# Batch 0 of a sparse-attention kernel: loads, casts and scores taken pair by pair, in one written order

## The chip, the cores and the metric

The kernel runs on one core of one Trainium2 chip. Its metric is device time in microseconds, the median of three runs. The core's engines are TensorE (PE, with its weight loads shown as PEld), VectorE (DVE), ScalarE (ACT), GpSimd (POOL) and SyncE (SP), which issues most of the DMAs. Each engine works through its own instructions in order; engines wait for one another by semaphores.

## The reference

Eight batches of eight heads, 576 tokens, 64 values a head, all float32. Heads 0 to 3 see the last 32 positions, heads 4 to 7 the earlier positions with the same remainder by 32. A feed-forward part without nonlinearity, but with a product of two branches, follows.

```python
scores = scale * np.matmul(q, k.transpose(0, 1, 3, 2))
mask_local = (rel >= 0) & (rel < stride)                       # heads 0..3, stride 32
mask_strided = (rel >= 0) & (pos[None, :] % stride == pos[:, None] % stride)   # heads 4..7
scores = np.where(masks, scores, -1e9)
attn = softmax(scores)                                         # max taken off, divided by the sum
attn_out = np.matmul(attn, v)                                  # (8, 8, 576, 64)
x = attn_out.transpose(0, 2, 1, 3).reshape(4608, 512)
out = ((x @ w1) * (x @ w2)) @ w3 @ w_out                       # 512 -> 1024 -> 1024 -> 512
```

## The kernel before

Work is cut into pairs of heads: 4 pairs in each of 8 batches, 32 in all. Pairs 0 and 1 of a batch are local (`s.local`, blocks of 96 queries, six of them), pairs 2 and 3 strided. In the first two batches (`AHEAD = 2`) strided pairs are in a "natural" layout (`s.nat`): token 4p+c is row p of block c, and the last 64 tokens (the "rest", loaded apart by `load_rest`) make a fifth block. For a pair the steps are:

- load q and k (`load_qk`: four heads, 512 KB a DMA, from SP), cast them to fp16,
- T1: four 128x128 PE transposes each for q and k (`ah_T1`), copied out of PSUM to `qT` by ACT and to `kT` by DVE (`ah_T1c`); `ah_R` does the rest of all pairs,
- scores in two groups. In batch 0 a bias matmul puts a large negative number where the mask is 0 (`ah_bias`, `biasL` and `biasN`), the score matmuls add to it (`ah_S0`), and ACT's exponential writes `ptm` or `nptm`. For natural pairs ACT also copies the last 16 columns to `emb` (`ah_tail`),
- PV (`ah_PV`): the weights times v with a column of ones, so that the sum comes along; `norm` on DVE takes a reciprocal of the sum and multiplies, for each of the two groups, into `xqs`,
- T2 (`ph_T2`): PE transposes of `xqs`, copied out to `xT` by ACT; for natural pairs DVE copies the last 64 columns.

Values: `load_vL` loads them for local pairs, casts them and copies 32 rows of each block's neighbour (the "halo") on POOL; `load_vN` does the strided ones. The columns of ones and the zero rows of `v16L` and `v16X` are memsets.

The feed-forward part works on tiles of 512 tokens. For each of eight column blocks jc, `a` makes x@w1 (PSUM tile `aps`, four matmuls over the four pairs' `xT`, ci = 0..3), ACT copies it to `asb`, `bb` makes x@w2 (`bps`), and DVE multiplies the two into `abt`. w3 and w_out are folded into one matrix on the core (`fold_tr`, `fold_tr2`: transposes of w3; `fold_mm`: the products, PSUM tile `ops`), so that one more matmul gives the output (`o_parts`). Weights are loaded by SP through the nine staging buffers of pool `stgp` and cast on POOL.

PE's order is written by hand: `pe(...)` holds an instruction in program order. For the other engines a scheduler places instructions, unless they are held too; `behind(x)` makes an instruction be issued after x. The list `stream` holds the steps of batch 0 in order, then those of batches 2 to 7 with gaps, which `host` fills with feed-forward work. In batch 0 before, T1, scores, PV and T2 of the four pairs are interleaved, and the first 16 `a` matmuls of the feed-forward part (four blocks, four ci) are set between the PV and T2 steps of the later pairs. Then come the `bb` matmuls of four blocks, the other blocks, the fold (with batch 1's steps at set places, `plan`), and from pair 8 on the batches of the `stream`. Pair 8 and 9 are the local pairs of batch 2.

PSUM is held by three pools: `psF` (three banks), `psB` (two tiles of two banks, for scores and shared `a` tiles) and `psM` (one bank). `warm(ps, n)` issues n 128x128 matmuls whose result nobody reads.

Of the kernel before, what the change touches and what calls it, by code (L numbers as in the profile page):

```python
# [19 lines left out]
def kernel(  # L20
# [64 lines left out]

    def copy(eng, out, in_):
        if eng == "a":
            return nc.scalar.copy(out=out, in_=in_)  # L88
        elif eng == "v":
            return nc.vector.tensor_copy(out=out, in_=in_)  # L90
        return nc.gpsimd.tensor_copy(out=out, in_=in_)  # L91
# [4 lines left out]
    make_identity(nc, id16)  # L96


# [6 lines left out]
    tmp2 = att.tile([P, 2 * S], FP16, tag="pte", bufs=2, name="tmp2")  # L105
    causal = tmp[:, 0:NW]
    nc.gpsimd.memset(causal, 1.0)
    nc.gpsimd.affine_select(out=causal, in_=causal, compare_op=ALU.is_ge,
                            fill=0.0, base=0, pattern=[[1, NW]], channel_multiplier=-1)
    setup["p"] = nc.gpsimd.affine_select(out=maskE[:, 0:P], in_=causal[:, 0:P], compare_op=ALU.is_ge,  # L110
                                         fill=0.0, base=31, pattern=[[-1, P]], channel_multiplier=1)
    nptms = [ffn.tile([P, 2, 2048], FP16, tag="abt", bufs=4, name="nptm0")]
    nc.gpsimd.memset(emb, 0.0)

    mps = psF.tile([P, 512], FP32, tag="f")
    sels = []
    for m, lo, n, w in ((8, 208, 18, P), (32, 352, 2, 64), (7, 0, 18, XW), (4, P, 18, YW)):
        sel = tmp[0:m, NW + lo:NW + lo + n * m]
        nc.vector.tensor_copy(out=sel.rearrange("r (t a) -> r t a", a=m),
                              in_=_ap(id16, 0, [[id16.ap[0][0], m], [0, n], [1, m]]))  # L120
        pe(nc.tensor.matmul(mps[0:w, lo:lo + n * m], sel[:, 0:w], sel, start=True, stop=True))
    for i in range(1, LT):
        lo = 0 if i == 1 else 32
        nc.vector.tensor_copy(out=maskE[:, QL[i] + lo:QL[i + 1] + 32], in_=maskE[:, lo:32 + QL[i + 1] - QL[i]])
    maskN = tmp2[:, 0:NQ]
    nc.vector.memset(maskN[:, NC * NW:NQ], 0.0)
    nc.vector.tensor_mul(maskN[:, 0:NW], mps[:, 208:208 + NW], causal)
    nc.vector.tensor_mul(maskN[0:64, NC * NW:NQ], mps[0:64, 352:416], causal[0:64, 0:64])
    nc.vector.tensor_copy(out=maskN[:, NW:NC * NW].rearrange("p (c x) -> p c x", x=NW),
                          in_=_ap(maskN, 0, [[maskN.ap[0][0], P], [0, NC - 1], [1, NW]]))  # L130
    nc.vector.tensor_copy(out=idw[:, P:2 * P - 32], in_=id16[:, 0:P - 32])
    biasL = tmp[:, S:2 * S]
    for bias, mask in ((biasL, maskL), (biasN, maskN)):
        nc.vector.tensor_scalar(out=bias, in0=mask, scalar1=1.0, scalar2=BIG, op0=ALU.subtract, op1=ALU.mult)
    nc.vector.memset(maskX[:, XC:S], 0.0)
    nc.vector.tensor_mul(maskX[:, 0:XW], mps[0:XW, 0:XW], causal[0:XW, 0:XW])
    nc.vector.tensor_mul(maskX[0:YW, XC:S], mps[0:YW, P:P + YW], causal[0:YW, 0:YW])
    setup["v"] = nc.vector.tensor_copy(out=maskX[:, XW:XC].rearrange("p (c x) -> p c x", x=XW),
                                       in_=_ap(maskX, 0, [[maskX.ap[0][0], XW], [0, XN - 1], [1, XW]]))


    v16L = [consts.tile([P, 4, LT, D + 1], FP16, name=f"v16L{i}") for i in range(2)]
    v16X = [consts.tile([P, 4, XN + 1, D + 1], FP16, name=f"v16X{i}") for i in range(2)]


    qT = consts.tile([P, 4, S], FP16)
    kT = consts.tile([P, 4, KW], FP16)
    ptms = [consts.tile([P, PTW], FP16, name=f"ptm{i}") for i in range(2)]
    nc.vector.memset(kT[:, :, S:KW], 0.0)
    for i in range(2):  # L150
        nc.vector.memset(v16L[i][:, :, :, D], 1.0)
        nc.vector.memset(v16L[i][LQ:P, :, LT - 1, 0:D], 0.0)
        nc.vector.memset(v16X[i][:, :, :, D], 1.0)
        nc.vector.memset(v16X[i][64:P, :, XN, 0:D], 0.0)
    for i in range(2):
        nc.vector.memset(ptms[i][:, S:640], 1.0)
        nc.vector.memset(ptms[i][:, 2 * S:PTW], 1.0)
# [26 lines left out]
    def load_w12(g):  # L184
        cs = bass.ds(g * 512, 512)
        for wd, wh in ((moe_w1, w1h), (moe_w2, w2h)):
            src = wd.rearrange("(c p) n -> p c n", p=P)
            for c in range(0, KM, 2):
                st = stgp.tile([P, 2, 512], FP32, tag="stg")
                nc.sync.dma_start(st, src[:, c:c + 2, cs])  # L190
                copy("p", wh[:, c:c + 2, cs], st)
# [10 lines left out]
    def load_qk(b, grp, engs="pp"):  # L202
        for nm, ten, eng in (("q", q, engs[0]), ("k", k, engs[1])):
# [4 lines left out]
            with behind(setup["p"] if b == 0 and grp == 0 else None):  # L208
                ins = copy(eng, t, st.rearrange("p h c d -> p c h d"))
            if b == 1:  # L210
                pe(ins)
            x16[(b, nm, grp)] = t

    def load_rest(b, eng="p"):
# [4 lines left out]
        with behind(setup["v"] if b == 0 else None):  # L219
            ins = copy(eng, t, st)  # L220
        if b == 1:
            pe(ins)
        x16[(b, "r")] = t

    def load_vL(b, hps=(0, 1)):
        vt = v16L[b % 2]
        for hp in hps:
# [4 lines left out]
            nc.gpsimd.tensor_copy(out=vt[0:LQ, hs, :, 0:D], in_=st[0:LQ])  # L232
            copy("p", vt[LQ:P, hs, 0:LT - 1, 0:D], vt[0:32, hs, 1:LT, 0:D])
# [58 lines left out]
    def ph_T(s, rest, pt):  # L292
# [18 lines left out]
        engs = (("a", qT), ("v" if s.local else "a", kT))  # L311

        def out():
            for i, (eng, t) in enumerate(engs):
# [48 lines left out]
    def ph_soft(s, pt):  # L363
# [8 lines left out]
        mask_mul(s, ptm[0:kr, PT0:PT0 + 2 * S], pte[0:kr], 0, S, 2)  # L372
# [14 lines left out]
    def ah_T1(s, i, dst=None):  # L387
        if dst is None:
            dst = psF.tile([P, 2 * NM], FP16, tag="f", name="tps")[:, 0:NM]
        src = x16[(s.b, "qk"[i], s.hp // 2)]  # L390
        h0 = 2 * (s.hp % 2)
# [61 lines left out]
    def ah_tail(s, g):  # L453
        t, w = ah_home(s)
        cs, lo, hi = ah_group(s, g)
        return nc.scalar.copy(out=_ap(emb, 640 * (s.hp - 2) + 130 * g, [[emb.ap[0][0], P], [256, 2], [65, 2], [4, 16]]),
                       in_=_ap(t, ah_off(s, g) + P, [[nptms[s.b].ap[0][0], P], [hi - lo, 2], [NW, 2], [1, 16]]))
# [32 lines left out]
    def ah_S0(s, gs, tails=True):  # L490
# [3 lines left out]
        for g in gs:  # L494
# [3 lines left out]
            if full is not None:  # L498
                nc.scalar.activation(out=o, in_=full[0:kr, :, 0:hi - lo], func=AF.Exp, bias=0.0, scale=scale)
# [41 lines left out]
    def norm(s, xv, c0, l):  # L541
# [3 lines left out]
        nc.vector.reciprocal(out=rcp[0:w, :, 0:l], in_=xv[:, :, :, D])  # L545
        nc.vector.tensor_mul(s.xqs[0:w, c0:c0 + l].rearrange("p i h d -> p h i d"), xv[:, :, :, 0:D],  # L546
                             _ap(rcp, 0, [[rcp.ap[0][0], w], [LT, 2], [1, l], [0, D]]))

    def ph_T2(s):
        n = s.n  # L550
        ps = psM.tile([P, 1024], FP16, tag="m")
# [9 lines left out]
        o = xT[s.hp][:, S * s.b:S * s.b + S]  # L561
        if s.local:
            copy("a", o, ps[:, 0:S])
        elif s.nat:
            nc.scalar.copy(out=o[:, 0:NM].rearrange("x (p c) -> x p c", c=4),  # L565
                           in_=ps[:, 0:NM].rearrange("x (c p) -> x p c", c=4))
            nc.vector.tensor_copy(out=o[:, NM:S], in_=ps[:, NM:S])
# [58 lines left out]
    def ab_parts(tch):  # L626
# [9 lines left out]
        def asb_copy(st):  # L636
            st["asb"] = ffn.tile([P, NT], FP32, tag="asb", name="asb")
            copy("v" if tch == 1 and st["a0"] else "a", st["asb"][:, 0:nt], st["a"][:, 0:nt])

        for jc in range(KF):  # L640
# [11 lines left out]
            def a(*cis, jc=jc, st=st, pool=psF, late=False):  # L652
                if cis[0] == 0:
# [4 lines left out]
                for ci in cis:  # L658
                    pe(nc.tensor.matmul(st["a"][:, 0:nt], w1h[:, ci, bass.ds(jc * P, P)], xT[ci][:, tok],  # L659
                                        start=(ci == 0), stop=(ci == KM - 1)))  # L660
                if cis[-1] == KM - 1 and not late:
                    asb_copy(st)

            def bb(*cis, jc=jc, st=st, pool=psF):
                if cis[0] == 0:
                    st["b"] = bank(pool, "bps")
                for ci in cis:
                    pe(nc.tensor.matmul(st["b"][:, 0:nt], w2h[:, ci, bass.ds(jc * P, P)], xT[ci][:, tok],  # L668
                                        start=(ci == 0), stop=(ci == KM - 1)))
                if cis[-1] == KM - 1:  # L670
# [91 lines left out]
    def fold_tr2(j0):  # L762
        pts = [psB.tile([P, 2, NB], FP32, tag="big", name=f"trp{j}").bitcast(FP16) for j in range(2)]
        for j in range(2):
            for kc in range(KF):
                for u in range(2):
                    r = half_rows(u)
                    pe(nc.tensor.transpose(pts[j][:, u, kc * 64:kc * 64 + 64], w3n[j0 + j][r, bass.ds(kc * P, P)],  # L768
                                           id16[r, r]))
        for j in range(2):  # L770
            copy("va"[j], fold_to(j0 + j, 0, DF).rearrange("x (c u r) -> x u c r", u=2, r=64),
                 pts[j][:, :, 0:KF * 64].rearrange("x u (c r) -> x u c r", r=64))
# [35 lines left out]
    def warm(ps, n):  # L808
        ps = ps.bitcast(FP32)[:, 256:384]
# [3 lines left out]
    def ah_Tw(s, i, n):  # L813
# [10 lines left out]
    add(ah_Ti, p0, 0)  # L824
    add(both, p0)
    add(ah_Ti, p0, 1)
    add(lambda: rest0.append(ah_R(0)))
    add(ah_S0, p0, (0,))
    add(ah_T, p1)
    add(lambda: rest0[0]())  # L830
    add(ah_S0, p0, (1,))
    add(ah_Tw, p2, 0, 4)
    add(both, p1)
    add(ah_S0, p1, (0, 1))
    add(ah_Ti, p2, 1)
    add(ah_Ti, p3, 0)
    add(ah_Tw, p3, 1, 4)
    add(both, p2)
    add(ah_S0, p2, (0, 1))
    add(ah_PV, p0, 0)  # L840
    add(ah_PV, p0, 1)
    add(both, p3)
    add(ah_S0, p3, (0, 1), False)
    add(ah_PV, p1, 0)
    add(ah_PV, p1, 1)
    add(ph_T2, p0)
    add(lambda: [pe(ah_tail(p3, g)) for g in range(2)])
    add(ah_PV, p2, 0)
    add(ah_PV, p2, 1)
    add(ph_T2, p1)  # L850
    add(lambda: a0(0, pool=psB))
    add(lambda: a1(0, pool=psB))
    add(ah_PV, p3, 0)
    add(ah_PV, p3, 1)
    add(lambda: a2(0, pool=psB))
    add(lambda: a3(0, pool=psB))
# [194 lines left out]
```

## Time and profile before

| | us |
|---|---|
| median of three runs (272.4, 272.41, 273.25) | 272.41 |
| the profiled execution | 271.57 |
| its span | 269.9 |
| PE busy | 258.7 (96%) |
| DVE / ACT / POOL busy | 155.9 / 140.6 / 99.2 |

The profile is of one execution. Its views used below: the page (shares of the whole span, groups of instructions by line), the windows (busy time in chosen stretches), the timeline (instructions in order of time, merged), the list of waits, and the chain (what the end is traced back to). Times are microseconds from the start of the span. A PE row's busy time is modelled from pipelined matmuls. Line numbers are those of the kernel before. The granted clock of the rows is 1.00 in nearly all windows.

### The profile page before, as it was taken

The numbers are of one execution on the slowest core, as the hardware profiler recorded it, in microseconds if no ns is written. First come the engines' busy times: TensorE is split into PE (matmuls) and PEld (weight loads), VectorE is DVE, ScalarE is ACT, GpSimd is POOL, SyncE is SP. The second block draws the span as 40 slices with busy tenths as digits, with TensorE's granted clock in tenths as the row PEclk, the third lists the DMA queues.
The fourth block names the chain that finished last, engine by engine and source line by source line (L and its number), as shares of the span: only waits on it lengthen the run. The fifth ranks groups of instructions, "written<-read, shape, count | busy, mean of one in ns | idle before, by whom it ended". The sixth has DMA issues, their size and how long they took to land.

```text
span 269.9 us, 6821 instructions
## 1 busy us (share of the span) xinstructions
PE 258.7 (96%) x2703; PEld 136.8 (51%) x2703; DVE 155.9 (58%) x370; ACT 140.6 (52%) x297; POOL 99.2 (37%) x119
## 2 busy tenths in 40 slices
PE   2899999999999999999999999999999999999994
PEld 1664465555555545555555555555455544444442
DVE  6362543365668776767676778677867753421320
ACT  2583434567647555556655555655556634333322
POOL 5487687788248205710850164027300000000000
PEclk9999999999999999999999999999999999999999
DMA  7899999798697449625943784398330012013003
GB/s 220 240 342 377 406 418 335 205 290 233 162 317 221 145 137 238 217 99 156 306 142 117 225 219 128 118 269 226 100 117 16 2 56 101 1 39 117 2 26 131
DMA packets 61100, 48.68 MB, mean 180 GB/s; under 512 B 31804, under 2 KB 52492, under 8 KB 61068
## 3 DMA queue, kind: packets, MB, share of 16 engines
q1 hardware_dynamic: 57036, 40.97, 50.2%
q10 hardware_dynamic: 4032, 7.28, 7.2%
q8 instruction: 21, 0.34, 0.5%
q14 instruction: 11, 0.09, 0.1%
HBM read 38.80 MB, written 9.44 MB: 179 GB/s over the span
## 4 chain that ended last, share of the span: by engine, by line
PE 94%; DMA 2%; ACT 1%; SPq 1%; DVE 1%; issue 0%; DVEq 0%
PE ops L711 28%; PE bps L668 23%; PE aps L659 23%; PE sps L383 3%; DMA st<-in_k_dram 2%; PE t2a L580 2%; PE pt L301 2%; PE sps L348 2%; PE tps L393 2%; PE sps L474 1%; PE sps L486 1%; PE ps L554 1%; PE xpl L531 1%; PE ops L739 1%; PE trp L768 1%; SPq L197 1%
## 5 line engine op out<-in xcount | busy, mean ns | idle before, releaser
L659 PE MATMUL aps<-xT,w1h 128*128 128x512 f16 (+1 forms) x288 | 73.7, 376 | 0.5 <-ACT xT L565 0.5
L668 PE MATMUL bps<-xT,w2h 128*128 128x512 f16 (+1 forms) x288 | 73.1, 376 | 0.6 <-ACT asb L88 0.6
L91 POOL CAST t<-st 128x1024 f16<-128x1024 f32 (+1 forms) x46 | 46.1, 1010 | 67.3 <-DMA st<-in_q_dram 53.0
L671 DVE TENSOR_TENSOR abt<-bps,asb 128x512 f16<-128x512 f32 (+1 forms) x72 | 48.6, 678 | 36.4 <-PE bps L668 34.8
L88 ACT COPY asb<-aps 128x512 f32<-128x512 f32 (+1 forms) x71 | 41.3, 584 | 51.9 <-PE aps L659 48.4
L711 PE MATMUL ops<-w,abt 128*128 128x512 f16 x280 | 67.1, 379 | 0.0
L668 PEld LDWEIGHTS <-w2h 128*128 128x128 f16 x288 | 27.1, 98 | 31.5 <-issue 1.3
L659 PEld LDWEIGHTS <-w1h 128*128 128x128 f16 x288 | 26.6, 98 | 29.2 <-issue 1.3
L711 PEld LDWEIGHTS <-abt 128*128 128x128 f16 x280 | 25.2, 98 | 26.2
L722 ACT COPY osb<-ops 128x512 f32<-128x512 f32 x35 | 21.0, 599 | 20.5 <-PE ops L711 20.5
L371 ACT ACTIVATE pte<-sps 128x1024 f16<-128x1024 f32 (+1 forms) x24 | 24.4, 1018 | 13.3 <-PE sps L348 12.8
L546 DVE TENSOR_TENSOR xqs<-sps,rcp 128x768 f16<-128x768 f32 (+1 forms) x24 | 21.4, 891 | 0.8
L360 DVE TENSOR_TENSOR ptm<-pte,maskE 128x1152 f16<-128x1152 f16 (+2 forms) x16 | 12.3, 771 | 7.9 <-ACT pte L371 7.6
L360 DVE TENSOR_TENSOR ptm<-pte,maskX 126x1152 f16<-126x1152 f16 x12 | 11.4, 946 | 7.7 <-ACT pte L371 7.7
L711 PE MATMUL ops<-woh,w3T 128*128 128x512 f16 x64 | 15.3, 380 | 0.0
L90 DVE COPY kT<-pt 128x512 f16<-128x512 f16 (+4 forms) x28 | 11.4, 416 | 6.5 <-ACT kT L88 4.7
L88 ACT COPY qT<-pt 128x224 f16<-128x224 f16 (+4 forms) x40 | 15.0, 424 | 0.2 <-PE pt L309 0.2
L232 POOL CAST v16L<-st 96x768 f16<-96x768 f32 x16 | 13.3, 830 | 3.0 <-DMA st<-in_v_dram 1.4
L383 PEld LDWEIGHTS <-ptm 128*128 128x128 f16 (+1 forms) x264 | 11.1, 98 | 6.0 <-DVE ptm L360 1.4
L260 POOL CAST v16X<-st 126x1024 f16<-126x1024 f32 x6 | 6.6, 1106 | 19.2 <-DMA st<-in_v_dram 19.2
L90 DVE COPY xT<-t2a 128x384 f16<-128x384 f16 (+1 forms) x22 | 8.5, 388 | 7.9 <-PE t2a L580 7.7
L91 POOL COPY v16L<-v16L 32x640 f16<-32x640 f16 x16 | 12.3, 773 | 1.0
(124 smaller groups left out, 275.7 us busy)
## 6 DMA issues: line engine op xcount, KB each, us to landing
st<-in_q_dram SPq DMA_DIRECT2D x16, 512.0 KB, 4.8
st<-in_k_dram SPq DMA_DIRECT2D x16, 512.0 KB, 5.6
st<-in_moe_w_dram SPq DMA_DIRECT2D x16, 512.0 KB, 9.9
out_dram<-osb ACTq DMA_DIRECT2D x27, 256.0 KB, 2.0
st<-in_v_dram SPq DMA_DIRECT2D x32, 144.0 KB
st<-in_v_dram SPq DMA_DIRECT2D x24, 112.0 KB, 2.5
st<-in_moe_w_out_dram SPq DMA_DIRECT2D x4, 512.0 KB, 12.0
out_dram<-osb SPq DMA_DIRECT2D x8, 256.0 KB, 4.2
```

The costliest lines, as they stand in the source:

```text
L88: return nc.scalar.copy(out=out, in_=in_)
L90: return nc.vector.tensor_copy(out=out, in_=in_)
L91: return nc.gpsimd.tensor_copy(out=out, in_=in_)
L360: nc.vector.tensor_mul(o.rearrange("p (a x) -> p a x", x=x), i.rearrange("p (a x) -> p a x", x=x), _ap(s.mask, lo, [[s.mask.ap[0][0], s.kr ...
L371: nc.scalar.activation(out=pv[0:kr, :, lo:hi], in_=src, func=AF.Exp, bias=0.0, scale=scale)
L383: pe(nc.tensor.matmul(s.ps[:, h, c * 65:c * 65 + 65], s.ptm[0:s.kr, c0:c0 + P], s.v[0:s.kr, 2 * (s.hp % 2) + h, c, :], start=True, stop=True))
L546: nc.vector.tensor_mul(s.xqs[0:w, c0:c0 + l].rearrange("p i h d -> p h i d"), xv[:, :, :, 0:D], _ap(rcp, 0, [[rcp.ap[0][0], w], [LT, 2], [ ...
L659: pe(nc.tensor.matmul(st["a"][:, 0:nt], w1h[:, ci, bass.ds(jc * P, P)], xT[ci][:, tok], start=(ci == 0), stop=(ci == KM - 1)))
L668: pe(nc.tensor.matmul(st["b"][:, 0:nt], w2h[:, ci, bass.ds(jc * P, P)], xT[ci][:, tok], start=(ci == 0), stop=(ci == KM - 1)))
L671: nc.vector.tensor_mul(abts[tch][:, jc, skip:], st["b"][:, 0:nt], st["asb"][:, 0:nt])
L711: pe(nc.tensor.matmul(st["ps"], lhs(ci), rhs(ci), start=(ci == 0), stop=(ci == KF - 1)))
L722: nc.scalar.copy(out=osb, in_=ps)
```

## The change

For batch 0, `load_first` loads q and k by pair of heads (256 KB a DMA: q0, k0, q1, k1, then the rest, then pairs 2 and 3); POOL casts the q halves, DVE the k halves and the rest (before: POOL and ACT, DVE the rest). The strided values are loaded between the two halves of the local ones; the second half's cast goes from POOL to ACT, after the exponentials and tails of pair 3, and its halo on POOL behind it. The memsets of ones and zeros go from DVE to POOL.

The mask set-up is put in one fixed order, and `biasN` and `maskX` are made between steps of pairs 0 and 1. All of batch 0 is one function, `batch0`, in which ACT's and DVE's instructions are held in program order too (`head`, `pin`). Scores, then PV and T2 of all four pairs come before the first `a` matmul; the order of PV is p0, p2, p3, p1, and T2 of pairs 0 and 3 get eight `warm` matmuls each. The 16 `a` matmuls stand behind it, with ci in the order 2, 3, 0, 1, and the weights' halves are loaded in that order.

Further edits: `fold_tr2` puts its 64-column transposes so that each PSUM tile holds one half of both blocks, with four copies of 512 columns for two of 1024, and moves between the two halves of a `fold_mm`. In `ph_soft` the mask product of pair 8 (`s.late`), and in `ph_T` the kT copy of pair 9, are issued after DVE's `asb` copy of the second tile's first block.

```diff
+    def load_first(hps):
+        grp = hps[0] // 2
+        for hp in hps:
+            h0 = 2 * (hp % 2)
+            for nm, ten in (("q", q), ("k", k)):
...
+                nc.sync.dma_start(st[:, h0:h0 + 2], ten[0, 2 * hp:2 * hp + 2, 0:NM].rearrange("h (p c) d -> p h (c d)", c=4))
+                x16[(nm, hp)] = t[:, hp % 2]
+                if nm == "q":
+                    pe(cast_first(nm, hp, "p"))
+
+    def cast_first(nm, hp, eng):
+        h0 = 2 * (hp % 2)
+        st = stage[(nm, hp // 2)][0]
+        return copy(eng, x16[(nm, hp)], st[:, h0:h0 + 2].rearrange("p h (c d) -> p c h d", c=4))
...
+            if b == 0 and hp == 1:
+                stage["v"] = cast
+                return
+            cast("p")
+            halo(b, hs)
...
-            for c in range(0, KM, 2):
+            for c in (2, 0) if g == 0 else (0, 2):
...
-        mask_mul(s, ptm[0:kr, PT0:PT0 + 2 * S], pte[0:kr], 0, S, 2)
+        s.late = lambda: mask_mul(s, ptm[0:kr, PT0:PT0 + 2 * S], pte[0:kr], 0, S, 2)
+        if s.hp or s.b > AHEAD:
+            s.late()
...
         o = xT[s.hp][:, S * s.b:S * s.b + S]
+        warm(ps, fill, 384)
...
-            nc.vector.tensor_copy(out=o[:, NM:S], in_=ps[:, NM:S])
+            copy("v", o[:, NM:S], ps[:, NM:S])
...
+    def batch0():
+        head[0] = True
+        cast_first("k", 0, "v")
+        both(p0)
+        T1(p0, 0)
+        T1(p0, 1)
+        to_bias(biasN, maskN)
+        ah_S0(p0, (0,))
+        cast_first("k", 1, "v")
+        make_maskX()
+        T1(p1, 0)
+        T1(p1, 1)
+        ah_bias(p1, 0)
+        ah_S0(p1, (0,))
+        copy("v", *stage["r"])
+        ah_R(0)()
+        ah_S0(p0, (1,))
+        ah_bias(p1, 1)
+        ah_S0(p1, (1,))
+        cast_first("k", 2, "v")
+        T1(p2, 0, 4)
+        T1(p2, 1)
+        T1(p3, 0)
+        both(p2)
+        ah_S0(p2, (0, 1), False)
+        cast_first("k", 3, "v")
+        T1(p3, 1, 4)
+        copy("v", idw[:, P:2 * P - 32], id16[:, 0:P - 32])
+        both(p3)
+        for g in range(2):
+            ah_tail(p2, g)
+        ah_S0(p3, (0, 1), False)
+        for g in range(2):
+            ah_tail(p3, g)
+        ah_PV(p0, 0)
+        ah_PV(p0, 1)
+        ah_PV(p2, 0)
+        ah_PV(p2, 1)
+        stage["v"]("a")
+        halo(0, slice(2, 4))
+        ph_T2(p0, psF, "f", 8)
+        ph_T2(p2)
+        ah_PV(p3, 0)
+        ah_PV(p3, 1)
+        ah_PV(p1, 0)
+        ah_PV(p1, 1)
+        ph_T2(p3, n=8)
+        ph_T2(p1, psF, "f")
+        head[0] = False
+
+    add(batch0)
+    for f in (a0, a1, a2, a3):
+        add(lambda f=f: f(2, pool=psB))
+    for ci in (3, 0):
+        for f in (a0, a1, a2, a3):
+            add(f, ci)
...
+    load_first((0, 1))
+    for i in range(2):
+        v_ones(i)
+    load_rest(0)
+    load_first((2, 3))
+    load_vL(0, (0,))
     load_vN(0)
+    load_vL(0, (1,))
+    stream[0]()
...
-            units += [lambda j=jc + 1: fold_tr2(j), h0, h1]
+            units += [h0, lambda j=jc + 1: fold_tr2(j), h1]
...
+        if i == 1:
+            with behind(setup["asb"]):
+                p8.late()
+                p9.late()
```

## The prediction

> **What bounds the kernel now.** I read the page first.
>
> ```profile
> span 269.9 us, 6821 instructions
> ...
> PE 258.7 (96%) x2703; PEld 136.8 (51%) x2703; DVE 155.9 (58%) x370; ACT 140.6 (52%) x297; POOL 99.2 (37%) x119
> ...
> ```
>
> TensorE (PE) is busy for 258.7 of 269.9 us. A busy share is no proof of full rate, but the table of stages (the windows view) shows that from 26 to 60 us PE is busy 34.00 of 34.00 us, and after that it loses 0.66 us between 60 and 80 us and 0.07 us up to 240. So the change can win only in the first 25 us, and at whatever stall those 0.66 us are; and anything that makes PE start its first long run of matmuls later is paid in full at the end. The timeline of the first 60 us comes next (start, duration, engine, what was done, and in brackets the idle time before it and who ended it).
>
> ```profile
> 4.66 1.04 POOL L91 CAST t<-st 128x1024 f16<-128x1024 f32 x1 [1.56 <-DMA st<-in_q_dram]
> ...
> 6.01 1.05 ACT L88 CAST t<-st 128x1024 f16<-128x1024 f32 x1 [3.93 <-DMA st<-in_k_dram]
> ...
> 8.94 0.68 DVE L90 COPY kT<-tps 128x512 f16<-128x512 f16 x1
> ...
> 10.06 1.04 PE L393 MATMUL tps<-idw,t 128*128 128x128 f16 x8
> ...
> 10.17 0.70 ACT L499 ACTIVATE ptm<-sps 128x640 f16<-128x640 f32 x1 [0.18 <-PE sps L474]
> ...
> 17.07 0.53 PE L474 MATMUL sps<-qT,kT 64*128 64x144 f16 x10
> ...
> 17.92 0.20 DVE L545 RECIPROCAL rcp<-xpl 128x6 f32<-128x6 f32 x1 [0.81 <-PE xpl L531]
> ...
> 18.15 0.56 DVE L546 TENSOR_TENSOR xqs<-xpl,rcp 128x384 f16<-128x384 f32 x1
> ...
> 21.36 0.56 DVE L546 TENSOR_TENSOR xqs<-xpl,rcp 128x384 f16<-128x384 f32 x1
> ```
>
> ```profile
> 22.14 0.58 ACT L565 COPY xT<-ps 128x512 f16<-128x512 f16 x1 [1.58 <-PE ps L554]
> ...
> 22.76 0.19 DVE L567 COPY xT<-ps 128x64 f16<-128x64 f16 x1 [0.84 <-ACT xT L565]
> ...
> 25.16 3.77 PE L668 MATMUL bps<-xT,w2h 128*128 128x512 f16 x16
> ...
> 49.97 0.61 PE L393 MATMUL tps<-idw,t 128*128 128x128 f16 x8
> ```
>
> Four things are to be seen. The first 512 KB of q are cast at 4.66 and the first 512 KB of k at 6.01, each when it lands. The exponentials of pair 0 begin at 10.17, the scores of pair 3 at 17.07, and the first `bps` matmul (w2's work, which stands behind all of batch 0) at 25.16: that last start is the date that counts. Eight 128-column transposes take 1.04 us at 10.06 and 0.61 us at 49.97: their spacing is 107 ns early and 56 ns later, so PE runs at half rate in the beginning although its row of the page says busy; the transposes of the trace keep the slow spacing until about 13 us. And one normalisation on VectorE (DVE) is a reciprocal of 0.20 us and a product of 0.56 us.
>
> The chain of waits says what set the last microseconds before 25.16, and, further on, the 0.66 us:
>
> ```profile
> 21.84 0.27 PE ps L554 x5
> ...
> 22.14 0.59 ACT xT L565
> ...
> 22.78 0.59 PE aps L659 x2
> ```
>
> ```profile
> 73.45 0.39 PE aps L659 x2
> ...
> 73.86 0.54 ACT asb L88
> ...
> 74.44 0.92 PE bps L668 x4
> ```
>
> Up to 25 us, T2 transposes, ScalarE's (ACT) copies of `xT` and the `aps` matmuls take turns; there are no longer gaps than 0.5 us, since `aps` matmuls stand between the PV and T2 groups. At 73.84 PE stops until ACT's copy of 0.54 us has freed a PSUM bank: it starts again at 74.44, where it could have gone on at about 73.7. The list of waits has it as 0.6 us.
>
> **Part 1: the head, up to the scores.** The first DMA before carries 512 KB; after, the first two (q and k of pair 0) carry as much together. So k of pair 0 lands when q's first half landed before, at 4.65, and not at 6.0. DVE's cast of 512 columns is 0.43 (row at 8.60), to 5.1; four transposes 0.61, to 5.7; the kT copy 0.68 (row at 8.94), to 6.45; eight score matmuls 0.45, to 7.0; exponentials 0.70, to 7.8. Before, they began at 10.17: three microseconds are won here. Most of it is given back at once, because everything behind is in a fixed order. Pair 1's kT copy ends at 8.6 (behind the second cast and maskX: 0.31 + 0.43 + 0.75 on DVE), its scores at 9.1, its exponentials at 9.9. The rest rows are cast by 8.95, transposed by 9.6, but ACT's copy of them (0.27) stands behind those exponentials, to 10.1; then PE does the second score groups (10.4 to 11.3), 16 transposes and fillers at 107 ns (1.7 us) and four bias matmuls (0.75), to 13.6. Scores of pair 2 at 13.6, two exponentials (0.65 + 0.75) to 15.3, which free the banks for pair 3's bias (0.35): pair 3's scores at 15.65 instead of 17.07. Of three microseconds 1.4 are left.
>
> The mask set-up is off the path: the DVE memsets of `v16L`/`v16X` (eight rows, 1.4 us) go to GpSimd (POOL), which waits for data there; if that cover were gone, they would hold the q cast of pair 2 (needed at 11.1, done at 8.9).
>
> **Part 2: the tail, from the first PV to `bps`.** Before, 16 `aps` matmuls filled PE while DVE normalised. After, all of `batch0` comes first, and the 16 `aps` matmuls (215 ns apart, 3.45 us; 4 take 0.86 in the chain) stand behind the last T2. So this stage is now a chain on DVE: eight normalisations. With 0.03 of overlap each, four local ones are 0.73, and of the four strided ones two are 0.58 (product 0.42) and two 0.72; together 5.5, with one 64-column xT copy 5.65. And DVE stops once: the order puts the xT copy of pair 2 (like the row at 22.76) ahead of pair 3's normalisation. It waits for ACT's copy, which waits for T2 of pair 2, which waits for pair 2's last product. Before, T2 at 21.68 to that copy at 22.76 was 1.08 us, with nothing of DVE behind it; here it is 1.15 us with four normalisations behind it, and PE behind those. First PV at 15.95, DVE from 16.35: 16.35 + 5.65 + 1.15 is 23.15, with start-up 23.3. The last T2 (0.3) ends at 23.6, the 16 `aps` at 27.1. Against 25.16 that is **1.9 us later**.
>
> I laid the groups of before out by the same durations, as a test of the method: `bps` came out at 25.2, against 25.16 in the trace.
>
> What else is in this stretch is covered. The 16 filler matmuls (0.9 us) stand where PE waits for DVE. ACT's cast of the second v half (0.8) ends at 18.6, the halo behind it at 19.4, PV of pair 1 needs it at 20.2; POOL idles in front of it from 15.4, and then casts w1 and w2 (four times 1.04) by 23.5, needed from 23.6 to 28.
>
> **Part 3: loads.** The smaller first DMAs need more issues: SyncE (SP) issued 512 KB in 0.44 and 0.49 us at the start, so four more cost at most 1.9 us of its queue, while the DMA share from 3 us on is above 1. SP's ninth weight load now waits for ACT's v cast (18.6; issued at 17.8 before), with eight 512 KB loads of about 1.3 us each queued: hidden. The weights may land up to 1 us earlier; PE comes 1.9 us later, so nothing is won by it. [...]
>
> **Part 4: later edits.** `fold_tr2` splits two copies of 1024 into four of 512 and moves between two halves of `fold_mm`: PE has no idle time there and gets 0.86 us of matmuls as cover. Zero; without cover ACT would pay 0.15 three times (0.58 twice against 1.01). The late mask of pair 8 and late kT copy of pair 9's transposes let DVE copy `asb` at about 73 us, before them, so that PE's bank is free at 73.6 and the 0.6 to 0.8 us stall goes. What is late next there is `aps` behind ACT's copy, due at 74.4, when PE arrives. I take -0.7; bounds 0 and -0.8.
>
> **Sum.** The profiled execution took 271.57 us, 1.7 more than its span. 271.57 + 1.9 - 0.7 = 272.8. The median of before's runs, 272.41, is 0.84 above that execution, so the runs should show 273.6: slower by 1.2 us, 0.45%. About 0.3% (0.8 us) is what a measurement of this kernel can tell from no change.
>
> **Bounds.** The one large unknown is when PE reaches full rate. By the same layout, three microseconds earlier gives `bps` at 25.9 (+0.7), three later 28.0 (+2.8); I take 13, where before had it, since PE's dense work begins only at 10.4 in both. Landings 0.4 earlier or later move it by 0.1 to 0.4; DVE's strided casts at 0.6 instead of 0.43 add 0.2.
>
> **Rivals.** *Faster: the tail is bound by PE's work and not by DVE.* From 15.95 PE has 60 PV matmuls at 30 ns (1.8), 22 T2 transposes (1.1), fillers 0.9, `aps` 3.45: `bps` at 23.2, 2.0 earlier; with part 4 -2.7, so 269.7 by the median; with half of DVE's chain hidden 271. For it speaks that the scores are 1.4 us early and that PE's work is less. Against it are the DVE rows, 5.65 us against 3.8 of PE. It decides in its favour if the eight normalisations take under 3.8 us, or if the xT copy of pair 2 doesn't hold them. Chance 0.20.
>
> *No difference: full rate comes at about 10 us,* because the first transposes already run at 4.5. Then +0.7 - 0.7, 272.4. In the trace, dense work from 6.6 to 8.0 and again from 9.1 did not bring it before 13. Chance 0.15.
>
> *Much slower: PE falls back to half rate in the tail,* where it has gaps of 0.5, 0.7 and 1.4 us. If it comes back after 4 us of dense work, as from 9.1 to 13 in the trace, nine `aps` have double spacing (as 107 is to 56) and seven 215: 5.4 instead of 3.45, and 275.5 by the median. In the trace full rate survives gaps of 0.5 us; longer ones aren't in it. [...] Chance 0.08, with full rate in the head only at 16 (274.5) in it.
>
> **Numbers.** The forecast has 0.57. Slower by over 0.3%: forecast and last rival, less the forecast's edge below 273.2, gives 0.62; the same 0.17; faster 0.21. The range 271.0 to 275.0 takes in the bounds and reaches into the faster case; it leaves out most of that and the far end of the last.
>
> **What would show it.** Right: exponentials of pair 0 near 7, scores of pair 3 near 15.7, DVE's xT copy of pair 2 after over 1 us of idle time, the last T2 near 23.4, `bps` near 27, and no PE wait at 74. Wrong: `bps` before 25.2, or T2 of pair 1 before 21.5; a 56 ns spacing of transposes before 12 us; `aps` at double spacing; or a new PE wait between 27 and 60 us, where I have none.

## The result, and the profile after

The changed kernel takes 275.02 us (median of five runs, 274.48 to 275.94) against 272.4 for the kernel before (271.88 to 273.25): 1.0111 times as long, 95% interval 1.008 to 1.0143. It is slower by 2.6 us where 1.2 was forecast, and lies just above the range of 271.0 to 275.0. The side was right, the size was not. The profiled execution is the one of 275.02, with a span of 273.1; before it was 271.57 and 269.9.

The page first:

```profile
span 273.1 us, 6865 instructions
...
PE 261.9 (96%) x2719; PEld 138.4 (51%) x2719; DVE 158.7 (58%) x369; ACT 140.3 (51%) x300; POOL 99.2 (36%) x127
```

PE is busy for 3.2 us more, as much as the span grew, though only 16 matmuls were added. As before, the busy row doesn't tell full rate from half. The timeline does (start, duration, engine, what was done, in brackets the idle time before it and its releaser; line numbers are now those of the changed kernel):

```profile
4.33 1.12 PE L531 MATMUL sps<-tmp,idw 128*128 128x320 f16 x4 [1.64 <-DVE tmp L144]
...
4.84 0.41 DVE L95 CAST t<-st 128x512 f16<-128x512 f32 x1
...
5.24 1.06 PE L438 MATMUL tps<-idw,t 128*128 128x128 f16 x8
...
6.34 0.69 DVE L95 COPY kT<-tps 128x512 f16<-128x512 f16 x1 [1.09 <-PE tps L438]
...
7.57 0.70 ACT L544 ACTIVATE ptm<-sps 128x640 f16<-128x640 f32 x1 [1.08 <-PE sps L519]
...
11.66 0.39 PE L519 MATMUL sps<-qT,kT 64*128 64x96 f16 x6
...
12.82 1.06 PE L438 MATMUL tps<-idw,t 128*128 128x128 f16 x8
...
13.67 1.27 PE L531 MATMUL sps<-biasN,idw 128*128 128x288 f16 x4
...
15.38 0.40 PE L438 MATMUL tps<-idw,t 128*128 128x128 f16 x4
...
17.00 0.53 PE L519 MATMUL sps<-qT,kT 64*128 64x144 f16 x10
...
17.86 0.20 DVE L590 RECIPROCAL rcp<-xpl 128x6 f32<-128x6 f32 x1 [1.30 <-PE xpl L576]
...
21.68 0.19 DVE L95 COPY xT<-t 128x64 f16<-128x64 f16 x1 [1.10 <-ACT xT L93]
...
28.35 3.77 PE L718 MATMUL bps<-xT,w2h 128*128 128x512 f16 x16
```

The first exponentials begin at 7.57 instead of 10.17: what the change is built for happens. But the scores of pair 3 begin at 17.00, where before had 17.07 and the forecast 15.65. Eight transposes still take 1.06 us at 12.82 (107 ns apart); only at 15.38 do four take 0.40 (56 ns apart). Full rate came at 15.05, not at 13. The chain of waits has the rest of the way to `bps`:

```profile
19.40 0.53 PE t L600 x6
...
20.52 1.14 ACT xT L93 x2
...
21.68 0.19 DVE xT L95
...
22.55 0.56 DVE xqs L591
...
24.56 0.39 PE t L600 x3
24.95 3.56 PE aps L709 x16
28.51 0.65 PE bps L718 x3
```

From first PV (17.46) to `bps` (28.35 in the timeline) it is 10.9 us; the forecast was 11.15. The tail is as predicted, and starts 1.5 us late. `bps` comes 3.2 us later than before's 25.16. The place of the old stall, the `bps` matmuls behind a pair of `aps` matmuls, stands at 77 us by now, and the chain runs through it without a stop:

```profile
76.67 0.38 PE aps L709 x2
77.05 0.88 PE bps L718 x4
```

Two new waits of PE appear after 80 us:

```profile
90.29 0.48 PE L425 MATMUL sps<-v16X,ptm 126*128 126x65 f16 x10 [0.26 <-DVE ptm L400]
```

```profile
114.65 1.02 PE L709 MATMUL aps<-xT,w1h 128*128 128x512 f16 x4 [0.20 <-DVE abt L721]
```

So the 3.2 us of span are 3.2 of `bps`, less the 0.62 of the old stall, plus 0.53 of idle PE after 80 us (in the table of stages, PE is busy 39.54 of 40.00 us from 80 to 120, where it was 40.00, and 79.86 of 80 from 120 to 200, where it was 79.93).

### The profile page after: what moved, and what is told of

Same layout as the page of the kernel before. It is cut to its first block, busy times and chain, and to the rows that moved or that the text cites. A ratio compares the mean times of both kernels' runs of the same rounds, so it can differ in the third digit from the quotient of the medians.

```text
span 273.1 us, 6865 instructions
## 1 busy us (share of the span) xinstructions
PE 261.9 (96%) x2719; PEld 138.4 (51%) x2719; DVE 158.7 (58%) x369; ACT 140.3 (51%) x300; POOL 99.2 (36%) x127
## 4 chain that ended last, share of the span: by engine, by line
PE 90%; DVE 5%; ACT 3%; issue 0%; POOL 0%; ACTq 0%; POOLq 0%
PE ops L761 28%; PE aps L709 22%; PE bps L718 21%; PE sps L425 3%; PE tps L438 2%; PE t2a L626 2%; PE sps L388 2%; PE pt L337 2%; PE sps L531 2%; DVE ptm L400 1%; PE sps L519 1%; ACT pte L411 1%; DVE xqs L591 1%; PE t L600 1%; PE trp L819 1%; DVE kT L95 1%
## 5 line engine op out<-in xcount | busy, mean ns | idle before, releaser
L709 PE MATMUL aps<-xT,w1h 128*128 128x512 f16 (+1 forms) x288 | 72.9, 376 | 0.3 <-DVE abt L721 0.2
L96 POOL CAST t<-st 128x1024 f16<-128x1024 f32 (+1 forms) x47 | 44.9, 964 | 60.8 <-DMA st<-in_q_dram 49.4
L718 PEld LDWEIGHTS <-w2h 128*128 128x128 f16 x288 | 27.1, 98 | 30.9 <-issue 0.7
L400 DVE TENSOR_TENSOR ptm<-pte,maskX 126x1152 f16<-126x1152 f16 x12 | 12.7, 1058 | 7.7 <-ACT pte L411 7.7
L96 POOL CAST v16L<-st 96x768 f16<-96x768 f32 x15 | 12.4, 826 | 11.2 <-DMA st<-in_v_dram 10.4
L425 PEld LDWEIGHTS <-ptm 128*128 128x128 f16 (+1 forms) x264 | 10.9, 98 | 6.7 <-DVE ptm L400 2.5
L96 POOL COPY v16L<-v16L 32x640 f16<-32x640 f16 x16 | 12.3, 768 | 4.9 <-ACT v16L L93 4.0
```

The lines of the kernel that those rows point to most:

```text
L400: nc.vector.tensor_mul(o.rearrange("p (a x) -> p a x", x=x), i.rearrange("p (a x) -> p a x", x=x), _ap(s.mask, lo, [[s.mask.ap[0][0], s.kr ...
L425: pe(nc.tensor.matmul(s.ps[:, h, c * 65:c * 65 + 65], s.ptm[0:s.kr, c0:c0 + P], s.v[0:s.kr, 2 * (s.hp % 2) + h, c, :], start=True, stop=True))
```

## The experiments

All ratios are to runs of the kernel before on the same chip.

**Does the late full rate hold the head?** 20 fillers in PE's first wait:

```diff
+    def hot(n):
+        for _ in range(n):
+            pe(nc.tensor.matmul(mps[:, 416:512], id16, id16[:, 0:96], start=True, stop=True))
+
+    hot(20)
     for i in range(1, LT):
         lo = 0 if i == 1 else 32
```

> The changed kernel with 20 more matmuls of 96 columns, read by nobody, set in PE's wait between the mask matmuls and the first bias matmuls (2.6 to 4.2 us); nothing else moves. Theory A (the head is late because PE is at half rate until about 15 us, and it is at half rate because its dense work begins late): the transposes' spacing is 56 ns from about 5.5 us on instead of from 15, the scores of pair 3 begin 1.5 to 2 us earlier than their 17.00, the first bps goes from 28.35 to about 26.5, and the time from 275.0 to about 273.1. Theory B (the casts and PSUM copies on DVE, ACT and POOL and the landings hold the head, PE's rate doesn't matter): the spacing may change, but bps moves by less than 0.5 and the time stays above 274.5.

275.44 us, ratio 1.0126 (1.0095 to 1.0157), `bps` at 28.32. The first four microseconds of gapless work changed nothing (PE's timeline):

```profile
2.62 1.78 PE L138 MATMUL mps<-idw 128*128 128x96 f16 x20
...
12.73 1.06 PE L443 MATMUL tps<-idw,t 128*128 128x128 f16 x8
...
15.35 0.40 PE L443 MATMUL tps<-idw,t 128*128 128x128 f16 x4
```

This didn't decide between the theories, because the rate itself didn't move: full rate came at 15.1 again. PE had worked almost without a gap from 1.85 to 6.0, and then stood for 1.0, 0.5 and 0.6 us in turn (worked out from the starts and columns of its matmuls). Either the rate is not set by PE's work, or this stretch of 4.15 us was not enough.

**All the waits filled.** Fillers in each long wait up to 11.6 us; the 20 of the run before stay. Those around the second score groups (`warm(k1, n)`) are written into a bank that is free by then:

```diff
         T1(p0, 1)
+        hot(10)
         to_bias(biasN, maskN)
...
-        T1(p1, 1)
+        k1 = T1(p1, 1)
         ah_bias(p1, 0)
+        hot(7)
         ah_S0(p1, (0,))
...
         ah_R(0)()
-        ah_S0(p0, (1,))
+        warm(k1, 2)
+        ah_S0(p0, (1,), fill=lambda: warm(k1, 4))
         ah_bias(p1, 1)
+        warm(k1, 2)
```

> The changed kernel with fillers in every long wait of PE up to 11.6 us: the 20 of the first filler run, 10 behind pair 0's transposes, 7 ahead of pair 1's scores, 8 around the second score groups; nothing else moves. In the first filler run PE was busy without a gap from 1.85 to 6.0 us and full rate still came at 15.1, after the first stretch of 3.5 us that had no gap from 11.6 on. Theory A (full rate comes at the end of the first stretch of a fixed grid of about 3.4 us in which PE has no gap, so after 3.4 to 6.8 us of work without gaps): 56 ns spacing of transposes by 8.7 us at the latest, the scores of pair 3 at 15.0 to 15.5 instead of 17.0, bps at 26.3 to 26.8, the time 273.1. Theory B (the rate is set by something else, such as the kind of matmul or the time since the start): the spacing stays 107 until about 15, bps at 28.3, the time 275.

273.13 us, ratio 1.0045 (1.0021 to 1.0068), clear of the changed kernel's interval. PE's timeline:

```profile
8.77 0.46 PE L138 MATMUL mps<-idw 128*128 128x96 f16 x7
...
12.08 0.61 PE L443 MATMUL tps<-idw,t 128*128 128x128 f16 x8
...
15.25 0.53 PE L526 MATMUL sps<-qT,kT 64*128 64x144 f16 x10
...
26.60 3.77 PE L725 MATMUL bps<-xT,w2h 128*128 128x512 f16 x16
```

The seven fillers at 8.77 are 42 ns apart (0.46 us with the last one's latency), the first after the change of rate at 8.5. Pair 3's scores come 1.75 us earlier, `bps` at 26.60 instead of 28.35, as theory A had it. So full rate at 8.5 instead of 15.05 is worth 1.75 us. It is not all that the head lost: the prediction's layout has `bps` at 25.9 with full rate at 10, and here it is at 26.60 with full rate at 8.5.

**What brings full rate, by itself.** 100 fillers back to back ahead of the head's work (`hot(100)`), run twice:

> The changed kernel with 100 fillers of 96 columns in place of 20, back to back from 2.6 us on, ahead of all other work of the head (which they delay): a direct measure of when full rate comes after gapless work. Theory A (a fixed grid of about 3.4 us, a stretch counts if PE has no gap in it): the spacing goes from 80 to 42 ns once, between 5.5 and 9.3 us (2.6 or 1.9 plus 3.4 to 6.8), at another place in another execution, and the rate then stays full. Theory B (a fixed amount of work or a fixed time after the first matmul): the same place in both executions, within 0.2 us.

> The same kernel in a second execution, for the place of the change of rate: theory A has it anywhere in 5.5 to 9.3 us, theory B where the first execution had it.

279.9 and 278.93 us; the fillers' delay is in them. The windows view of the fillers alone, in the first execution and then in the second (from:to, length, PE's busy time and in brackets the number of matmuls that touch the stretch, then DVE's, the granted clock, the DMA share and GB/s):

```profile
5.00:6.00 1.00, 1.00 (x16) 0.00 (x0) 1.00 0.76 224
6.00:7.00 1.00, 1.00 (x16) 0.00 (x0) 1.00 1.00 276
7.00:8.00 1.00, 1.00 (x16) 0.00 (x0) 1.00 1.12 344
8.00:9.00 1.00, 1.00 (x25) 0.00 (x0) 1.00 1.03 350
```

```profile
5.00:6.00 1.00, 1.00 (x17) 0.00 (x0) 1.00 0.90 239
6.00:7.00 1.00, 1.00 (x28) 0.00 (x0) 1.00 0.80 212
```

The same program went to full rate at 8.17 us in one execution and at 5.85 in the other: theory B is out. Theory A is half right, for the rate did not stay. In the second execution's PE timeline:

```profile
11.04 0.33 PE L524 MATMUL sps<-qT,kT 64*128 64x96 f16 x8 [0.79 <-DVE kT L95]
...
13.04 0.45 PE L524 MATMUL sps<-qT,kT 64*128 64x96 f16 x8 [0.44 <-DVE kT L95]
...
16.57 1.06 PE L443 MATMUL tps<-idw,t 128*128 128x128 f16 x8
...
19.62 0.39 PE L867 MATMUL tps<-idw 128*128 128x128 f16 x4
```

The same eight scores take 0.33 at 11.04 and 0.45 at 13.04; full rate is back at 19.5. In the first execution four scores at 14.59 still take 0.26, four transposes at 16.50 take 0.61, and full rate is back near 21.8 (ten scores take 0.75 at 19.39 and 0.53 at 22.00). So from one rise to the next it is 13.65 and about 13.6 us, with the fall about halfway: at 12.6 to 13.0 in one, at 14.8 to 15.5 in the other. These equal steps fit a fixed grid, of 6.8 us as well as of theory A's 3.4. That 3.4 us is an estimate from the dense work ahead of full rate in the changed kernel (11.6 to 15.05) and in the run of 20 fillers (11.6 to 15.1); no change was seen 3.4 us after another.

I worked out PE's busy share from the starts and columns of its matmuls. It is 81% from 9.25 to 12.66, at whose end the kernel before has full rate (the bias matmul of 256 columns at 12.67 takes 273 ns, the one at 7.10 took 417), and 90% from 11.6 to 15.05 in the changed kernel; there, 53% from 8.2 to 11.6 brought no rise. Full rate was lost after stretches in which PE was busy for about a third (8.9 to 13.0 us in the second execution, 11.0 to 15.5 in the first; an estimate from the counts of the rows and the full-rate spacings), and was kept in the changed kernel's own tail at 46% (17.4 to 24.9). So dense work stood before these rises and thin work before these falls. How dense it must be, and for how long, no run shows.

**Do the change's own fillers hold the rate?** All 24 of them left out (`T1(p2, 0)`, `T1(p3, 1)`, and T2 of pairs 0 and 3 without eight each):

> The changed kernel without its 24 filler matmuls (4 in each of two T1 steps, 8 in each of two T2 steps). Theory A (PE's rate goes by some 3.4 us of work before, and idle stretches up to 0.8 us don't bring it back; the fillers only cost PE time in the head): the aps matmuls keep 215 ns, the scores of pair 2 come 0.3 to 0.4 earlier, bps at 28.0, the time 274.6. Theory B (the fillers hold PE's rate): full rate comes later than 15 us or is lost in the tail, with transposes 107 ns apart or aps matmuls 430 ns apart after 20 us, and the time is 275.5 or more.

275.75 us, ratio 1.0128 (1.0093 to 1.0163): no difference from the changed kernel that these runs resolve, though the number is the one that theory B named; theory A's 3.4 us is the estimate above. `bps` is at 28.21, and the 16 `aps` keep their 3.63 us. Full rate came at 15.9, later than 15.05, but other kernels with this head had 15.1 to 17.2 with their fillers. In the tail, full rate held without the fillers; in the head they can't be told from the difference between executions (5.85 and 8.17 in the two above).

**DVE's stop in the tail.** Pair 2's xT copy behind pair 3's normalisations:

```diff
-        ph_T2(p2)
+        later = []
+        ph_T2(p2, later=later)
         ah_PV(p3, 0)
         ah_PV(p3, 1)
+        later[0]()
```

> The changed kernel, with DVE's 64-column xT copy of pair 2 put behind both normalisations of pair 3 instead of ahead of them. Theory A (the tail is a chain on DVE, and this copy stops it for 1.1 us): DVE has no idle time above 0.3 us between its first and its last normalisation, the last T2 ends about 1.0 earlier (23.9 for 24.95), bps begins at 27.3, the time is 274.0. Theory B (the tail is held by PE's order, PSUM banks or POOL's casts of the weights, and DVE's stop is covered): bps moves by less than 0.3.

274.24 us, ratio 1.0085 (1.0056 to 1.0114); by time alone it can't be told from the changed kernel. The profile can, although `bps` by itself moved by only 0.09, as in theory B: it is at 28.26 although this execution's first PV came at 17.92 (full rate at 16.85), so the tail is 10.34 us for 10.89, 0.55 shorter. Half of the stop was cover for another. DVE's timeline:

```profile
20.49 0.56 DVE L591 TENSOR_TENSOR xqs<-xpl,rcp 128x384 f16<-128x384 f32 x1
21.58 0.18 DVE L590 RECIPROCAL rcp<-xpl 128x4 f32<-128x4 f32 x1 [0.54 <-PE xpl L576]
```

DVE now waits 0.54 us for pair 3's PV, which PE's order puts behind T2 of pair 2, which waits for DVE's last product.

**Matmuls for the tail's gaps.** Eight of the 16 `aps` are moved between the steps, and eight fillers go:

```diff
         ah_PV(p1, 0)
+        for f in (a0, a1, a2, a3):
+            f(2, pool=psB)
         ah_PV(p1, 1)
-        ph_T2(p3, n=8)
+        ph_T2(p3)
+        for f in (a0, a1, a2, a3):
+            f(0)
         ph_T2(p1, psF, "f")
...
     for f in (a0, a1, a2, a3):
-        add(lambda f=f: f(2, pool=psB))
-    for ci in (3, 0):
-        for f in (a0, a1, a2, a3):
-            add(f, ci)
+        add(f, 3)
```

> The changed kernel with eight of the 16 first aps matmuls put between the tail's steps, as before had them: four between the two PV groups of pair 1, four between T2 of pair 3 and T2 of pair 1 (in place of eight fillers); their weights' loads are the same. Theory A (after the last T2 PE has 3.45 us of matmuls that could have been done in its waits of 0.77, 0.23, 0.4 and 0.4 us and in the fillers' place): the last T2 stays near 24.9, the bps after it comes 1.7 earlier, at 26.7, the time 273.2. Theory B (those matmuls then delay PV and T2, on which DVE's chain hangs, as much as they save): bps at 28 or later, the time 274.5 or more.

272.82 us, ratio 1.002 (0.9998 to 1.0041). PE's timeline:

```profile
22.10 1.02 PE L709 MATMUL aps<-xT,w1h 128*128 128x512 f16 x4
...
23.74 1.03 PE L709 MATMUL aps<-xT,w1h 128*128 128x512 f16 x4
...
25.29 1.90 PE L709 MATMUL aps<-xT,w1h 128*128 128x512 f16 x8
27.03 3.77 PE L718 MATMUL bps<-xT,w2h 128*128 128x512 f16 x16
```

From first PV (17.87) to `bps` it is 9.16 us instead of 10.89: 1.73 less, as theory A had it.

**The three together:**

> The changed kernel with the three edits together: the fillers of all head waits, the xT copy of pair 2 behind pair 3's normalisations, eight aps matmuls spread in the tail. If the three causes (late full rate, DVE's stop, aps behind the last T2) are separate, their gains add: 1.9 + 0.6 + 1.7, bps at 24.2, the time 270.8, below before's 272.4. If they are one cause seen three times, or the casts of the weights on POOL (done at 24.5 in the changed kernel) take over, bps stays above 25.5 and the time above 272.

270.17 us, ratio 0.9937 (0.9914 to 0.9961): faster than before and after. In PE's timeline `bps` begins here:

```profile
24.10 3.77 PE L731 MATMUL bps<-xT,w2h 128*128 128x512 f16 x16
```

The three add up (1.75 + 0.55 + 1.73 from 28.35 is 24.3), so they are three separate causes.

**One more step,** pair 3's first PV ahead of T2 of pair 2 on PE:

> The kernel of the three edits, with the first PV group of pair 3 put ahead of T2 of pair 2 on PE. In the three edits' profile DVE still stops for 0.54 us between pair 2's and pair 3's normalisations, because PE does T2 of pair 2, which waits for DVE, before pair 3's PV. Theory A (DVE's chain still ends the tail): that stop goes, bps at 23.6 instead of 24.1, the time 269.6. Theory B (PE's work is the end of the tail by now): bps stays at 24.0 to 24.2 and the time at 270.2.

```profile
23.65 3.77 PE L731 MATMUL bps<-xT,w2h 128*128 128x512 f16 x16
```

`bps` comes 0.45 earlier, but the head of this execution was as much earlier too: from first PV (15.05) to `bps` it is 8.60 us, as in the three edits (15.50 to 24.10). DVE's stop went from 0.54 to 0.15 us and the end of the tail did not move: theory B. The time, 270.72 (0.9943, 0.9916 to 0.9969), is no better.

**The late edits alone,** on the kernel before (mask product of pair 8, kT copy of pair 9):

> The kernel before, with only the late mask product of pair 8 and the late kT copy of pair 9. Theory A: PE's wait of 0.62 us at 74 us goes and nothing comes for it: 0.6 less, 271.8. Theory B (the late mask product brings the two new waits that the changed kernel has at 90 and 114 us, 0.26 and 0.20): 0.6 less 0.5, so 272.3, and those waits show about 3 us earlier than in the changed kernel.

270.51 us, ratio 0.9945 (0.9918 to 0.9971). PE's `bps` row that stood at 74.44 with a wait of 0.62 has none now, and the first `bps` comes earlier too:

```profile
23.84 3.77 PE L676 MATMUL bps<-xT,w2h 128*128 128x512 f16 x16
...
72.46 0.92 PE L676 MATMUL bps<-xT,w2h 128*128 128x448 f16 x4
```

PE is busy all 40.00 us from 80 to 120, so the late edits by themselves don't bring the two new waits. The gain, 1.3 us by the medians, is more than the 0.6 of the stall; the interval reaches down to 0.8. In this execution the other part is the head, in which nothing was edited: `bps` is at 23.84 where the kernel before had 25.16, and full rate came at 10.15 and not at 12.7. So one profile of this head can differ from another by 1.3 us. Whether the medians differ for the same reason stays open.

This run is also the measure for the three edits together. Their 0.9937 and the 0.9945 of the late edits alone, which they contain, can't be told apart, and their `bps` at 24.10 is no earlier than 23.84. That the new head and tail, even with the three repairs, gain anything over the late edits is not shown.

**The late edits with 36 fillers in the head of before:**

> The kernel before with the late mask product and kT copy, and 36 fillers of 128 columns in PE's waits of the first 9 us. With theory A of the fillers, full rate comes by 8.5 us in every execution instead of at 10.2 (late edits alone) or 12.9 (before): bps at 23.8 to 24.3, the time 270.0 and with less scatter than the late edits alone (268.9 to 273.4). With theory B the fillers change nothing: the time is that of the late edits alone, 270.5, with the same scatter.

270.69 us, ratio 0.9961 (0.994 to 0.9982): not told apart from the late edits alone. Full rate came at 10.15 and not by 8.5; gaps of 0.2 to 0.3 us were left, and `bps` is at 24.97, behind a wait of 0.66 us for POOL's cast of w1. The forecast of theory A was wrong here, and the scatter (269.4 to 272.5) is not much smaller.

**Where the two new waits come from.** Behind them are mask products on DVE of 1.22 and 1.40 us instead of 0.76, with POOL's casts and copies beside them:

```profile
89.01 1.22 DVE L400 TENSOR_TENSOR ptm<-pte,maskX 126x1152 f16<-126x1152 f16 x1 [0.64 <-ACT pte L411]
...
112.47 1.40 DVE L400 TENSOR_TENSOR ptm<-pte,maskX 126x1152 f16<-126x1152 f16 x1 [0.72 <-ACT pte L411]
```

One more POOL copy behind each exponential from pair 8 on:

```diff
+        nc.gpsimd.tensor_copy(out=biasN[0:kr, 0:S], in_=pte[0:kr, S:2 * S])
         s.late = lambda: mask_mul(s, ptm[0:kr, PT0:PT0 + 2 * S], pte[0:kr], 0, S, 2)
```

> The changed kernel with one more copy on POOL (576 columns of the exponentials into a tile that is no longer used) behind each exponential of the pairs from 8 on, so that it starts when DVE's mask product of that pair starts. Theory A (DVE's product of two SBUF operands and a POOL instruction hold each other up): the mask products, 0.76 us where POOL was idle beside them, take 1.2 to 1.4 in most of the 24 pairs, PE gets more waits on them, and the time rises by 1 to 5 us. Theory B (POOL and DVE do not meet, the products of 1.22 and 1.40 had another cause): the products keep 0.76 in most pairs and the time stays within 0.5 of 275.0.

275.39 us, one run. The numbers are theory B's: 18 of 24 products kept 0.76, and the time is within 0.5 of 275.0. But its reason, that POOL and DVE do not meet, is wrong, for the copies were held up: they took 0.67 in seven cases and about 1.2 in 17, as in these two pairs of the timeline:

```profile
107.33 0.76 DVE L400 TENSOR_TENSOR ptm<-pte,maskE 128x1152 f16<-128x1152 f16 x1 [0.79 <-ACT pte L411]
...
109.18 0.67 POOL L412 COPY biasN<-pte 128x576 f16<-128x576 f16 x1
...
113.75 0.76 DVE L400 TENSOR_TENSOR ptm<-pte,maskX 126x1152 f16<-126x1152 f16 x1 [0.78 <-ACT pte L411]
...
113.85 1.19 POOL L412 COPY biasN<-pte 126x576 f16<-126x576 f16 x1 [0.70 <-ACT pte L411]
```

Here the one that starts second is held up: the copy took 1.19 us behind a product that began 0.10 us before it, and 0.67 where it began 1.1 us after the product had ended. Over twelve profiles, the products of pairs 8 and later with nothing on POOL beside them took 747 to 761 ns (124 of them), those that began before POOL's instruction, or within 60 ns of its end, 757 to 760 (59), and those that found a POOL instruction running 757 to 1644 (105, median 996); what such a product lost was about what was left of POOL's instruction, less 0.15 us. So the long products come from when POOL's batch work happens to fall. The delay of the change doesn't decide that. From 80 to 240 us PE is idle for 0.60 us in the changed kernel, but for 0.00 and 0.07 in the runs without fillers and with the late xT copy, which have `bps` at 28.21 and 28.26; and it is idle for 0.34 and 1.08 in the three edits together and with all waits filled, where `bps` is early (24.10 and 26.60). That these 0.5 us are a cost of the change is not shown.

## Why the prediction was right and wrong, step by step

- **The head's gain, and "the mask set-up is off the path".** Three microseconds up to the first exponentials, 2.6 measured: they begin at 7.57, where the forecast had 7.0. One step that failed is the mask set-up, taken as free. DVE is at the masks almost without a pause until its cast of k at 4.84 (4.65 in the forecast), and PE's first bias matmuls wait for DVE's set-up until 4.33. Pair 0's q transposes stand behind these matmuls in PE's order, so eight transposes (1.06 us) and not four (0.61) lie between k's cast and its copy. The fixed order carries the 0.6 us on: pair 1's kT copy ends at 9.2 for 8.6, and the second score groups at 12.0 for 11.3. In the run without fillers the masks end 0.4 us sooner and the first exponentials begin at 7.20, but pair 1's cast of k then waits for its load until 7.62, and the second score groups end no earlier (12.3). So two things hold the head here, and the forecast had neither. This is read from profiles; no run took either away.
- **"I take 13, where before had it, since PE's dense work begins only at 10.4 in both."** This is the other step that failed, and the one that the runs tested. PE is dense only from 11.6, and in six kernels with this head (one with 20 more fillers, one without the change's own) full rate came at 15.05, 15.1, 15.9, 16.7, 16.85 and 17.2. The transposes and bias matmuls behind the second score groups, 2.3 us in the forecast, took 2.9, since the bias matmuls ran at half rate too (1.2 for 0.75). With the 0.7 from the step before, pair 3's scores came 1.35 later than forecast. By the prediction's own bounds full rate at 15.05 puts `bps` at 27.7 (between its 27.1 for 13 and 28.0 for 16); the rest of the measured 28.35 is about the 0.7 of the step before. The 13 was read from one execution, and the pairs leave PE more waits: in the changed kernel's profile PE is busy for 53% from 8.2 to 11.6 and for 65% from 9.6 to 13.0, where it was busy for 81% and 90% ahead of full rate in the two kernels. That full rate at 13 was out of reach with this head is an estimate from these shares, since no run shows where the limit lies. How much later it comes differs between executions: 15.05 to 17.2 in these six, and by 2.3 us in the two of one program.
- **DVE's chain and its stop.** From DVE's first reciprocal to the end of the last T2, 7.25 us forecast, 7.1 measured; the stop 1.15 against 1.10. Right, but the stop by itself is worth 0.55.
- **The `aps` behind the last T2,** 3.45: 3.46 measured, of which half could have stood in PE's gaps (1.73 won).
- **Loads and POOL's weight casts hidden.** PE has no wait for either in the changed kernel. Right for this execution; in the run without fillers DVE's cast of pair 1's k waits 0.30 us for its load.
- **Part 4, the stall at 74.** 0.7 taken, 0.62 measured. Right.
- **No new wait later.** None came between 27 and 60 us, but 0.53 us after 80, which the prediction put at nothing without looking beyond 60. The other runs have between 0.00 and 1.08 us there; what decides it in this execution stays open.
- **From one execution to the runs.** 0.84 was added because before's profiled execution lay under its median; after's is its median. So the profiles differ by 3.45 us and the medians by 2.6. Against the sum for the profile, 272.8, the miss is 2.2 us; that it is only 1.4 against 273.6 is luck.
- **The rivals.** *Tail bound by PE*: the chain runs through DVE, so no. *Full rate at 10*: never with this head without more fillers; with them at 8.5 it is still 1.0045. *PE falls back to half rate in the tail*: not here: behind waits of 0.58, 0.77, 0.23 and 0.38 us the 16 `aps` still took 3.63. What a wait of 1.4 us would have done is not shown; in the second execution with 100 fillers the rate was lost behind waits of 0.60 and 0.79 us.

## What to carry to other kernels

Look for the date at which the transposes' spacing halves (107 to 56 ns here, at 15.05 us), and count back: a head that is cut finer starts its first work earlier and can still end later, because full rate comes late where PE has waits (15.05 here, 8.5 with the waits filled). Filling those waits with matmuls that nobody reads paid 1.75 us here; filling the first wait alone paid nothing. Before moving matmuls behind a chain on another engine, lay them in that chain's gaps: the change took 16 of them out, and setting eight back won 1.7 us. And measure the small edits of a large change by themselves: as far as these runs tell, the two late ones alone gave what the whole change gave after three repairs.

## What the runs showed of the hardware

- The granted clock of the windows reads 1.00 in stretches where transposes are 107 ns apart as well as where they are 56: it does not show the half rate of the head.
- The date of full rate differs between executions of one program by 2.3 us (5.85 and 8.17), and full rate was lost again in both, 6.8 to 7.2 and 6.6 to 7.3 us after it had come, after stretches in which PE was busy for about a third.
- Loads land at different dates too: with the same DVE order and the same loads, DVE's cast of batch 0's rest rows stood at 8.60 in the kernel before, waiting for its load, and at 7.22 with the late edits alone. A head is best read from more than one profile.
